# A two-layer attention and SwiGLU kernel: SyncE's DMA queue written in program order, weight loads set by the release of their slots, and the first half chunk's q and k evacuated straight into SBUF

## The chip, the cores and the metric

The kernel runs on one core of a Trainium2 chip. A core has TensorE (PE, matmuls), VectorE (DVE), ScalarE (ACT), GpSimd (POOL) and SyncE (SP, which here only issues DMA transfers). The metric is device time in microseconds (us), as a median of several executions. Spans inside a profile are about 1.8 us shorter than the time of the same execution. "Granted clock" is the share of TensorE's full clock that the profile shows as granted, 1.00 being all of it.

## The reference

Two layers. Each has a windowed attention (8 keys per token at distances 0, 2, ... 14; 32 heads of 32) and a SwiGLU block. S = 2048 tokens, D = 1024, F = 3584, all bf16.

```python
def _A_ref(x, wqkv, wo):
    qkv = (x @ wqkv).reshape(B, S, 3, H, Dh)          # then split into q, k, v
    logits = einsum("bhsd,bhswd->bhsw", q, k[idx]) * scale   # idx = pos - 2*w, masked below 0
    o = einsum("bhsw,bhswd->bhsd", softmax(logits), v[idx])
    return o.reshape(B, S, D) @ wo
def _B_ref(x, w1, w3, w2):
    return (silu(x @ w1) * (x @ w3)) @ w2
x = x + _A_ref(_layernorm(x), wqkv, wo);  x = x + _B_ref(_layernorm(x), w1, w3, w2)   # twice
```

## The kernel before

Tokens are handled in four chunks of 512 (`c`), and the attention in eight halves of 256 per layer (`h`). The engines share the work thus:

- TensorE computes q, k, v (`ps`, 8 tiles of 8 matmuls for each of q, k and v of a chunk), the output projection (`po`), gate and up (`pg`, `pu`) and the down projection (`acc`).
- ScalarE evacuates `ps`, which means that it copies the result out of the matmuls' accumulator into a staging tile `sgt`; SyncE stores `sgt` to DRAM and loads q, k, v of each half back as `qT`, `kT`, `vT`.
- VectorE does the attention itself: products with shifted copies of k, a tree of additions, softmax, products with shifted copies of v, giving `oT`. It also does layer norm statistics, residual additions and the SwiGLU product.

The instruction order of TensorE, VectorE and ScalarE is fixed by the program. The program keeps a small model of the three engines' times (`now`), and places background work of VectorE, and the `po` tiles, where that model believes their inputs ready. In the kernel before, the order of SyncE's queue is left to the scheduler of the framework. The code below is shortened, with comments added.

```python
ctx.enter_context(tc.manual_schedule(engines={PE, DVE, Activation}))      # SP is not in it
wp   = tile_pool(name="wp", bufs=8)      # 8 weight slots of 1 MB
qkvp = tile_pool(name="qkvp", bufs=1)    # qT, kT, vT: one buffer each
psum = tile_pool(name="psum", bufs=8)
...
def attention_steps():                   # a generator: each step is (cost, ready time, emit)
    for g, (l, h) in enumerate(halves):
        load_qk(l, h)                    # loads qT, kT if q and k of the chunk are stored
        while (l, h) not in qks: yield "blocked"; load_qk(l, h)
        load_v(l, h)                     # does nothing while v of the chunk is not stored
        ...                              # q*k products, softmax, At
        if g + 1 < len(halves): load_qk(*halves[g + 1])
        load_v(l, h)
        ...                              # At*v products -> oT
        oT_at[l, h] = now["dve"]
def between(hold, must=False):           # called between groups of TensorE's tiles
    while o_queue and (must or oT_at.get(half_of(o_queue[0]), 1e9) + 0.3 <= now["pe"]):
        o_tile()                         # 16 po matmuls
        if not must: break
...
for c in range(NCH):                     # the first layer's q, k, v
    for which in range(3):
        if c == NCH - 1 and which == 0: o_queue += [(0, n) for n in range(TPC)]
        if c == NCH - 1 and which == 2: between(False, True)     # the forced place
        q_part(0, c, which)
```

## Time and profile before

The time is 1634.05 us (median of 3, 1633.86 to 1635.31).

| what | value |
|---|---|
| span of the profiled execution | 1632.6 us |
| TensorE busy | 1614.9 us (99%) |
| VectorE busy | 1175.1 us (72%) |
| first `ps` matmul | 14.09 us |
| first `pg` matmul | 206.06 us |
| first attention product on VectorE | 60.08 us |

TensorE sets the time. The first lines below are the page's table of busy time by engine. The line after the dots is from its table of groups: line, engine, operation, output and inputs, shapes and count, then the busy time and mean ns of one, then the idle time before the group. "Busy" alone does not tell that TensorE runs at its peak. The count does, in the table of 25 us windows further down: 117 or 118 matmuls per full window, one each 0.216 us.

```profile
PE 1614.9 (99%) x7479; PEld 801.0 (49%) x7479; DVE 1175.1 (72%) x1960; ACT 351.9 (22%) x542; POOL 1.9 (0%) x12
...
L535 PE MATMUL pg<-xnT,w1t 128*128 128x512 bf16 x1792 | 423.3, 379 | 0.0
```

The table of windows of the kernel before: start and end of the window, its length, then busy us (and instructions) of PE, of the weight loads, of DVE, ACT and POOL, then the granted clock of TensorE, the DMA engines' busy share and GB/s.

```profile
150.00:175.00 25.00, 24.46 (x114) 15.42 (x113) 23.72 (x41) 9.30 (x17) 0.00 (x0) 1.00 0.43 117
175.00:200.00 25.00, 17.95 (x70) 8.70 (x69) 20.88 (x38) 3.60 (x7) 0.00 (x0) 0.80 0.71 227
200.00:225.00 25.00, 25.00 (x117) 12.60 (x116) 24.36 (x39) 8.53 (x12) 0.00 (x0) 1.00 0.76 234
```

The window from 175 to 200 us has 70 matmuls in place of 117, and a clock of 0.80. From 206 us on there is no listed wait of TensorE. The timeline of TensorE shows what happens there (start, duration, engine, line, operation, shapes, count, and in brackets the idle time before it and what ended it):

```profile
175.14 0.81 PE L466 MATMUL po<-wo,oT 128*128 128x512 bf16 x3
177.35 0.39 PE L466 MATMUL po<-wo,oT 128*128 128x512 bf16 x1 [1.41 <-DVE oT L317]
179.75 0.61 PE L466 MATMUL po<-wo,oT 128*128 128x512 bf16 x1 [2.01 <-DVE oT L317]
182.15 0.61 PE L466 MATMUL po<-wo,oT 128*128 128x512 bf16 x1 [1.79 <-DVE oT L317]
184.55 7.85 PE L466 MATMUL po<-wo,oT 128*128 128x512 bf16 x26 [1.79 <-DVE oT L317]
192.25 13.98 PE L500 MATMUL ps<-xnT,wqkv 128*128 128x512 bf16 x64
206.06 1.89 PE L535 MATMUL pg<-xnT,w1t 128*128 128x512 bf16 x8
```

TensorE reaches the `po` tiles of the second half and finds `oT` coming slice by slice from VectorE, 2.4 us apart. After that, 26 `po` matmuls take 7.85 us where 26 x 0.216 = 5.6 us would do: the clock had fallen. VectorE is late because it started late. These are the first three lines of the view of its waits between 14 and 206 us (what waited, for what: us in total, times, longest). The first of them lies mostly before the attention; the other two interrupt or delay it:

```profile
DVE rstd L202 <- ACT sd L195: 20.6, 7, 16.8
DVE pr L370 <- DMA kT<-qkv_d_1_127: 12.0, 1, 12.0
DVE xn L215 <- DMA xnT<-xn: 5.1, 2, 2.5
```

### The profile page before, as it was taken

The numbers are of one execution on the slowest core, as the hardware profiler recorded it, in microseconds if no ns is written. First come the engines' busy times: TensorE is split into PE (matmuls) and PEld (weight loads), VectorE is DVE, ScalarE is ACT, GpSimd is POOL, SyncE is SP. The second block draws the span as 40 slices with busy tenths as digits, with TensorE's granted clock in tenths as the row PEclk, the third lists the DMA queues.
The fourth block names the chain that finished last, engine by engine and source line by source line (L and its number), as shares of the span: only waits on it lengthen the run. The fifth ranks groups of instructions, "written<-read, shape, count | busy, mean of one in ns | idle before, by whom it ended". The sixth has DMA issues, their size and how long they took to land.

```text
span 1632.6 us, 18984 instructions
## 1 busy us (share of the span) xinstructions
PE 1614.9 (99%) x7479; PEld 801.0 (49%) x7479; DVE 1175.1 (72%) x1960; ACT 351.9 (22%) x542; POOL 1.9 (0%) x12
## 2 busy tenths in 40 slices
PE   8999899999999999999999999999999999999999
PEld 5666444444444644456444554445544444444444
DVE  3689899889998998999979848984489843122222
ACT  4332221204011331213222123022230212011110
POOL 0000000000000000000000000000000000000000
PEclk9999899999999999999999999999999999999999
DMA  9744664556646856477554674638675355445440
GB/s 313 223 126 129 194 194 146 166 168 191 186 154 180 258 158 180 142 220 247 154 169 143 200 252 143 181 129 256 222 183 163 123 178 168 142 143 180 155 129 27
DMA packets 337114, 286.33 MB, mean 175 GB/s; under 512 B 69632, under 2 KB 319488, under 8 KB 336896
## 3 DMA queue, kind: packets, MB, share of 16 engines
q1 hardware_dynamic: 336736, 284.59, 57.0%
q8 instruction: 58, 0.95, 0.2%
q10 hardware_dynamic: 288, 0.52, 0.1%
q14 instruction: 32, 0.26, 0.1%
HBM read 239.99 MB, written 29.36 MB: 165 GB/s over the span
## 4 chain that ended last, share of the span: by engine, by line
PE 94%; DVE 5%; DMA 1%; ACT 0%; issue 0%; ACTq 0%; DVEq 0%
PE acc L560 24%; PE pu L543 24%; PE pg L535 24%; PE ps L500 16%; PE po L466 6%; DVE pr L370 1%; DVE tm L429 1%; DVE pr L315 1%; DVE tm L315 1%; DMA xnT<-xn 0%; DVE psmT L393 0%; DVE L L395 0%; DMA x_sb<-in_A_x_dram 0%; DVE psm L317 0%; DVE st_133 L244 0%
## 5 line engine op out<-in xcount | busy, mean ns | idle before, releaser
L535 PE MATMUL pg<-xnT,w1t 128*128 128x512 bf16 x1792 | 423.3, 379 | 0.0
L543 PE MATMUL pu<-xnT,w3t 128*128 128x512 bf16 x1792 | 423.3, 379 | 0.0
L560 PE MATMUL acc<-w2t,hT 128*128 128x512 bf16 x1792 | 390.8, 379 | 0.0
L500 PE MATMUL ps<-xnT,wqkv 128*128 128x512 bf16 x1536 | 333.0, 379 | 2.3 <-ACT sgt L504 1.9
L539 ACT ACTIVATE sg<-pg 128x512 bf16<-128x512 f32 x224 | 133.7, 597 | 790.3 <-PE pg L535 755.7
L547 DVE TENSOR_TENSOR hT<-sg,pu 128x512 bf16<-128x512 bf16 x224 | 152.9, 683 | 209.9 <-PE pu L543 195.2
L543 PEld LDWEIGHTS <-w3t 128*128 128x128 bf16 x1792 | 175.3, 98 | 211.5
L560 PEld LDWEIGHTS <-hT 128*128 128x128 bf16 x1792 | 175.3, 98 | 211.5
L535 PEld LDWEIGHTS <-w1t 128*128 128x128 bf16 x1792 | 175.4, 98 | 211.4
L500 PEld LDWEIGHTS <-wqkv 128*128 128x128 bf16 x1536 | 220.4, 143 | 114.0 <-issue 2.9
L370 DVE TENSOR_TENSOR pr<-qT,kT 128x2048 bf16<-128x2048 bf16 x128 | 156.5, 1222 | 75.5 <-DMA kT<-qkv_d_1_130 61.2
L504 ACT CAST sgt<-ps 128x512 bf16<-128x512 f32 x192 | 109.1, 588 | 228.0 <-PE ps L500 195.8
L429 DVE TENSOR_TENSOR tm<-At,vT 128x2048 bf16<-128x2048 bf16 x128 | 156.2, 1220 | 2.4
L567 DVE TENSOR_TENSOR x_sb<-x_sb,acc 128x512 bf16<-128x512 bf16 x128 | 87.1, 681 | 91.4 <-PE acc L560 91.4
L315 DVE TENSOR_TENSOR pr<-pr 128x1024 bf16<-128x1024 bf16 (+1 forms) x256 | 134.4, 552 | 0.4
L315 DVE TENSOR_TENSOR tm<-tm 128x1024 bf16<-128x1024 bf16 (+1 forms) x256 | 133.4, 552 | 0.2
L466 PE MATMUL po<-wo,oT 128*128 128x512 bf16 x512 | 118.7, 384 | 7.0 <-DVE oT L317 7.0
L466 PEld LDWEIGHTS <-oT 128*128 128x128 bf16 x512 | 50.4, 99 | 69.9 <-DVE oT L317 9.3
L190 DVE BATCH_NORM_STATS2 st<-x_sb 128x6 f32<-128x512 bf16 x120 | 76.0, 671 | 0.3 <-DMA x_sb<-in_A_x_dram 0.3
L471 DVE TENSOR_TENSOR x_sb<-x_sb,po 128x512 bf16<-128x512 bf16 x64 | 43.3, 684 | 21.4 <-PE po L466 20.8
L539 ACT ACT_TABLE_LOAD x31 | 39.8, 1283 | 57.2 <-PE pg L535 57.1
L393 DVE STREAM_TRANSPOSE psmT<-psm 128x2048 bf16<-128x2048 bf16 x16 | 36.9, 2309 | 0.4
(160 smaller groups left out, 370.1 us busy)
## 6 DMA issues: line engine op xcount, KB each, us to landing
w1t<-in_B_w_dram SPq DMA_DIRECT2D x56, 1024.0 KB, 5.3
w3t<-in_B_w_dram SPq DMA_DIRECT2D x56, 1024.0 KB, 7.4
w2t<-in_B_w_dram SPq DMA_DIRECT2D x48, 1024.0 KB, 5.4
wqkv<-in_A_wqkv_dram SPq DMA_DIRECT2D x28, 1024.0 KB, 6.1
w2t<-in_B_w_dram SPq DMA_DIRECT2D x16, 512.0 KB, 5.1
qkv_d_0_126<-sgt SPq DMA_DIRECT2D x16, 256.0 KB, 2.8
qkv_d_1_127<-sgt SPq DMA_DIRECT2D x16, 256.0 KB, 5.3
qT<-qkv_d_0_126 SPq DMA_DIRECT2D x8, 512.0 KB, 4.8
```

Of the source, the lines that this page charges most:

```text
L315: nc.vector.tensor_tensor(b[:, 0:m, :], b[:, 0:m, :], b[:, m:2 * m, :], op=ALU.add)
L370: V.tensor_tensor(pr[:], qT[:], kT[:, :, k0:k0 + TCH], op=ALU.mult)
L429: V.tensor_tensor(tm[:], At[:], win, op=ALU.mult)
L466: nc.tensor.matmul(ps[:], lhsT=oT[:, t, j * P:(j + 1) * P], rhs=wo[:, t, hh * 512:(hh + 1) * 512], start=(t == 0), stop=(t == KT - 1))
L500: nc.tensor.matmul(ps[:], lhsT=ws[kk // KH][:, kk % KH, t::KT], rhs=xnT[:, kk, :], start=(kk == 0), stop=(kk == KT - 1))
L504: nc.scalar.copy(sgt[:, t - t0, :], ps[:])
L535: nc.tensor.matmul(pg[:], lhsT=w1t[:, kk, fi * P:(fi + 1) * P], rhs=xnT[:, kk, :], start=(kk == 0), stop=(kk == KT - 1))
L539: nc.scalar.activation(sg[:], pg[:], ACTF.Silu)
L543: nc.tensor.matmul(pu[:], lhsT=w3t[:, kk, fi * P:(fi + 1) * P], rhs=xnT[:, kk, :], start=(kk == 0), stop=(kk == KT - 1))
L547: nc.vector.tensor_tensor(hT[:, f - f0, :], sg[:], pu[:], op=ALU.mult)
L560: nc.tensor.matmul(acc[:], lhsT=hT[:, f - f0, j * P:(j + 1) * P], rhs=w2ts[(f - f0) // 8][:, (f - f0) % 8, :], start=(f == f0), stop=(f == ...
L567: nc.vector.tensor_tensor(xs, xs, acc[:], op=ALU.add)
```

## The change

Its intent: let the first attention begin as soon as k is computed, without a trip of q and k through DRAM, and keep SyncE's queue free of waits that hold other transfers back. There are also a fourth `xn` buffer (paid for by letting `L` and `An`, and `m4` and `e4`, share memory), other expected arrival times of x, and a first x tile that is split over two queues. Shortened to its core, with comments added:

```diff
-    ctx.enter_context(tc.manual_schedule(engines={PE, DVE, Activation}))
+    ctx.enter_context(tc.manual_schedule(engines={PE, DVE, Activation, SP}))
-    x_at = [12.5] + [20.0 + 10 * c for c in range(1, NCH)]
+    x_at = [12.5, 22.0, 27.0, 36.0]
-    for j in range(TPC):
-        (nc.scalar if j % 2 else nc.sync).dma_start(x_sb[:, j:j + 1, :], xin[:, j:j + 1, :])
+    for j, queue in ((0, nc.sync), (1, nc.sync), (TPC - 1, nc.scalar), (2, nc.sync)):
+        for h in range(2 if j == 0 else 1):        # tile 0 in two halves, one per queue
+            ...
+    seq = [...]        # all weight tiles, in the order of their use
+    def load_weight(pieces=1): ...                 # next tile of seq, on SyncE's queue
+    def release(n): due.extend([None] * n)         # after a tile's last matmul
+    def flush():                                   # first thing in between()
+        while due: due.pop(); load_weight()
 def q_part(...):
+        first = (l, c) == (0, 0) and which < 2
+        if first: now_T = qkvp.tile(..., name="kT" if which else "qT"); ...
                 nc.scalar.copy(sgt[:, t - t0, :], ps[:])
+                if first:
+                    nc.scalar.copy(now_T[:, t, HALO if which else 0:], ps[:, 0:TCH])
...
-    load_wqkv(0, 2)
-    load_x(1)
-    load_wqkv(1)
-    load_wqkv(2)
+    for i in range(4):                             # the weights of q and k
+        load_weight(1 if i > 1 else 2)
+    load_x(1)
...                                                # v's weights, x of chunks 2 and 3: inside q of chunk 0
             if c == 1 and which == 1:
-                nc.sync.dma_start(wo[:], wo_v)
+                then = (lambda: nc.sync.dma_start(wo[:], wo_v),)
```

More of the change, by code (lines that the diff above doesn't have):

```diff
@@ L65 @@
     wp = ctx.enter_context(tc.tile_pool(name="wp", bufs=8))
-    xnp = ctx.enter_context(tc.tile_pool(name="xn", bufs=3))
+    xnp = ctx.enter_context(tc.tile_pool(name="xn", bufs=4))
     xtp = ctx.enter_context(tc.tile_pool(name="xnT", bufs=2))
@@ L77 @@
     ctx.enter_context(tc.manual_schedule(engines={mybir.EngineType.PE, mybir.EngineType.DVE,
-                                                  mybir.EngineType.Activation}))
+                                                  mybir.EngineType.Activation, mybir.EngineType.SP}))
     MM, TABLE, DMA = 0.216, 1.3, 2.5
@@ L160 @@
     x_sb = const.tile([P, S // P, D], BF16, name="x_sb")
-    for j in range(TPC):
-        (nc.scalar if j % 2 else nc.sync).dma_start(x_sb[:, j:j + 1, :], xin[:, j:j + 1, :])
+    for j, queue in ((0, nc.sync), (1, nc.sync), (TPC - 1, nc.scalar), (2, nc.sync)):
+        for h in range(2 if j == 0 else 1):
+            w_ = D // (2 if j == 0 else 1)
+            (nc.scalar if h else queue).dma_start(x_sb[:, j, h * w_:(h + 1) * w_], xin[:, j, h * w_:(h + 1) * w_])
     hT = const.tile([P, HTN, CH], BF16, name="hT")
@@ L376, in attention_steps @@
             psmT = smp.tile([P, W * NE, 4], BF16, name="psmT", tag="tr")
-            L = smp.tile([P, W, NE], FP32, name="L")
-            m4 = smp.tile([P, 4, NE], FP32, name="m4")
+            L = smp.tile([P, W, NE], FP32, name="L", tag="L")
+            m4 = smp.tile([P, 4, NE], FP32, name="m4", tag="m4")
             mx = smp.tile([P, NE], FP32, name="mx")
             E = smp.tile([P, W, NE], BF16, name="E")
-            e4 = smp.tile([P, 4, NE], FP32, name="e4")
             sm_ = smp.tile([P, NE], FP32, name="sm_")
@@ L384, in attention_steps @@
             rsb = smp.tile([P, NE], BF16, name="rsb")
-            An = smp.tile([P, W, NE], BF16, name="An")
             at = {}
@@ L401, in attention_steps @@
             yield 0.72, 0.0, exps
+            e4 = smp.tile([P, 4, NE], FP32, name="e4", tag="m4")
+            An = smp.tile([P, W, NE], BF16, name="An", tag="L")
             yield 0.46, at["E"], lambda: V.tensor_tensor(e4[:], E[:, 0:4, :], E[:, 4:8, :], op=ALU.add)
@@ L440, with load_weight @@
     KH = KT // 2
-    wq_held = {}
-    def load_wqkv(which, pieces=1):
-        halves = []
-        for h in range(2):
+    NW = 8
+    seq = [("qkv", which, h) for which in range(3) for h in range(2)]
+    for u in range(len(units)):
+        for f0, f1 in fsplits:
+            for g0 in range(f0, f1, FG):
+                seq += [("w1", g0, min(FG, f1 - g0)), ("w3", g0, min(FG, f1 - g0))]
+            seq += [("w2", g0, min(8, f1 - g0), hh) for hh in range(2) for g0 in range(f0, f1, 8)]
+        if 1 <= u and u + 3 < len(units):
+            seq += [("qkv", which, h) for which in range(3) for h in range(2)]
+    w_tiles, due, used = [], [], [0]
+    def load_weight(pieces=1):
+        if len(w_tiles) == len(seq):
+            return
+        kind, i, n, *rest = seq[len(w_tiles)]
+        if kind == "qkv":
             w = wp.tile([P, KH, D], BF16, name="wqkv", tag="w")
@@ L450, in load_wqkv, with weight, release @@
                 nc.sync.dma_start(w[:, k0:k0 + step, :],
-                                  wqkv_v[:, h * KH + k0:h * KH + k0 + step, which * D:(which + 1) * D])
-            halves.append(w)
-        wq_held[which] = halves
+                                  wqkv_v[:, n * KH + k0:n * KH + k0 + step, i * D:(i + 1) * D])
+        elif kind == "w2":
+            w = wp.tile([P, 8, 512], BF16, name="w2t", tag="w")
+            nc.sync.dma_start(w[:, 0:n, :], w2_v[:, i:i + n, rest[0] * 512:(rest[0] + 1) * 512])
+        else:
+            w = wp.tile([P, KT, FG * P], BF16, name=kind + "t", tag="w")
+            v = w1_v if kind == "w1" else w3_v
+            nc.sync.dma_start(w[:, :, 0:n * P], v[:, :, i * P:(i + n) * P])
+        w_tiles.append(w)
+    def weight(kind):
+        w = w_tiles[used[0]]
+        assert seq[used[0]][0] == kind
+        used[0] += 1
+        return w
+    def release(n):
+        due.extend([None] * n)
+    def flush():
+        while due:
+            due.pop()
+            load_weight()
     o_queue, norm_queue = [], []
@@ L477, in between @@
     def between(hold, must=False):
+        flush()
         while o_queue and (must or oT_at.get((o_queue[0][0], o_queue[0][1] // 2), 1e9) + 0.3 <= now["pe"]):
@@ L488, in ready_norm, with q_part @@
         return xnT_at[key]
-    def q_part(l, c, which):
+    firsts = []
+    def q_part(l, c, which, ws, then=()):
         ready = ready_norm(("Q", l, c))
         xnT = xnTs[("Q", l, c)]
-        ws = wq_held[which]
+        first = (l, c) == (0, 0) and which < 2
+        if first:
+            now_T = qkvp.tile([P, KT, TCH + (HALO if which else 0)], BF16, name="kT" if which else "qT")
+            firsts.append(now_T)
+            if which:
+                nc.vector.memset(now_T[:, :, 0:HALO], 0.0)
         for t0 in range(0, KT, SG):
@@ L505, in q_part @@
                 done = act(0.6, r)
+                if first:
+                    nc.scalar.copy(now_T[:, t, HALO if which else 0:], ps[:, 0:TCH])
+                    done = act(0.4)
             nc.sync.dma_start(qkv_d[l][which][:, t0:t0 + SG, c * CH:(c + 1) * CH], sgt[:])
             between(False)
+            if then and t0 // SG < len(then):
+                then[t0 // SG]()
         qkv_at[l, c, which] = done + DMA / 2
+        if len(firsts) == 2:
+            qks[0, 0] = firsts[0], firsts[1], done + 0.1
+            firsts.append(None)
     def b_stage(u, hold):
@@ L519, in b_stage @@
                 gn = min(FG, f1 - g0)
-                w1t = wp.tile([P, KT, FG * P], BF16, name="w1t", tag="w")
-                nc.sync.dma_start(w1t[:, :, 0:gn * P], w1_v[:, :, g0 * P:(g0 + gn) * P])
-                w3t = wp.tile([P, KT, FG * P], BF16, name="w3t", tag="w")
-                nc.sync.dma_start(w3t[:, :, 0:gn * P], w3_v[:, :, g0 * P:(g0 + gn) * P])
+                w1t, w3t = weight("w1"), weight("w3")
                 for fi in range(gn):
@@ L528, in b_stage @@
                         between(hold)
+                    else:
+                        flush()
                     if f == 8 and 1 <= u and u + 3 < len(units):
@@ L548, in b_stage @@
                     th = dve(0.64, r)
+                release(2)
             for hh in range(2):
-                w2ts = []
-                for g0 in range(f0, f1, 8):
-                    gn = min(8, f1 - g0)
-                    w2t = wp.tile([P, 8, 512], BF16, name="w2t", tag="w")
-                    nc.sync.dma_start(w2t[:, 0:gn, :], w2_v[:, g0:g0 + gn, hh * 512:(hh + 1) * 512])
-                    w2ts.append(w2t)
+                w2ts = [weight("w2") for g0 in range(f0, f1, 8)]
                 for j in range(TPC):
@@ L570, in b_stage @@
                         nc.sync.dma_start(xout[:, n, hh * 512:(hh + 1) * 512], xs)
+                    if j == TPC - 1:
+                        release(2)
                     between(hold and not lastsplit, lastsplit and hh == 0 and j == 1 and not hold)
@@ L578 @@
     xnT_at["Q", 0, 0], norm_left["Q", 0, 0] = now["pe"], 0
-    load_wqkv(0, 2)
+    for i in range(4):
+        load_weight(1 if i > 1 else 2)
     load_x(1)
-    load_wqkv(1)
-    load_wqkv(2)
-    for r in range(R):
-        queue_norm(("Q", 0, 1), 1, r)
+    queue_norm(("Q", 0, 1), 1, 0)
+    queue_norm(("Q", 0, 1), 1, 1)
+    for c in (2, 3):
+        for r in range(R):
+            queue_norm(("Q", 0, c), c, r, (norm_stats,))
     for c in range(NCH):
@@ L590 @@
                 between(False, True)
-            q_part(0, c, which)
-            if c == 0 and which < 2:
-                load_x(2 + which)
-                for r in range(R):
-                    queue_norm(("Q", 0, 2 + which), 2 + which, r, (norm_stats,))
+            then = ()
+            if c == 0 and which == 0:
+                then = (lambda: load_x(2), load_weight, load_weight, lambda: load_x(3))
+            if c == 1 and which == 0:
+                then = (load_weight, load_weight)
             if c == 1 and which == 1:
-                nc.sync.dma_start(wo[:], wo_v)
+                then = (lambda: nc.sync.dma_start(wo[:], wo_v),)
+            q_part(0, c, which, w_tiles[2 * which:2 * which + 2], then)
+            if c == NCH - 1:
+                release(2)
             if which == 0 and 1 <= c < NCH - 1:
@@ L600 @@
                     queue_norm(("Q", 0, c + 1), c + 1, r, (norm_apply,))
+    used[0] = 6
     for u, (l, c) in enumerate(units):
@@ L609 @@
             for which in range(3):
-                load_wqkv(which)
                 if which == 2:
                     between(False, True)
-                q_part(*units[q], which)
+                q_part(*units[q], which, [weight("qkv"), weight("qkv")])
+                release(2)
 _INS = ['A_x', 'A_wqkv', 'A_wo', 'B_x', 'B_w1', 'B_w3', 'B_w2']
```

## The prediction

> **What bounds the kernel now.** TensorE. The page's busy table gives it 99% of the 1632.6 us span. From the first `pg` matmul (206.06 us, timeline of PE) to the end, no wait of PE is listed, and the table of 25 us windows shows 117 or 118 matmuls in every window after 200 us: one per 0.216 us. The Trainium skill ("TensorE: Matmul & The Clock Gate", phases on the wall clock) states 215.7 ns for a warm 512-column matmul; this trace agrees, so nothing is to be gained after 206 us.
>
> What can be gained lies before 206 us:
> - Head: the first `ps` matmul starts at 14.09 us. VectorE waits 3.9 us for the first x tile (view of waits); the serial norm chain runs from there.
> - 14.09 to 206.06 is 191.97 us, with 768 `ps` and 64 `po` matmuls: 832 x 0.216 = 179.7 us. So 12.3 us are lost. The view of waits names `po <- DVE oT` 7.0 us in 4 waits (177 to 185 us), `ps <- ACT sgt` 1.9 us (98 and 154 us). The rest, about 3 us, is the clock: in windows of 4 us the granted clock is 0.79, 0.50, 0.50, 0.93 between 176 and 192 us. The same page (HAM oscillation) warns of idle gaps over 3.4 us; here four of 1.4 to 2.0 us sufficed.
>
> **What the change does.**
> 1. q and k of the first half chunk go straight to SBUF. Before, VectorE sat 12.0 us until `kT` returned from DRAM, started attention at 60.08 us, broke off for 6.6 us of statistics, and lost 5.1 us to `xn` waiting for the transposes. From 60.08 to 185.07 (second half's `oT`) is 125 us, so 113 us without those two. Now k's last tile is copied about 28.7 us after the first `ps` matmul, near 42 us, with all statistics done in the idle time before. The second `oT` then ends near 155 us; the forced `po` tiles need it near 171 us. The wait goes, and its throttling.
> 2. Cost: 16 more ScalarE copies of 128x256, about 0.4 us each (estimated from the 0.59 us copy). ScalarE then does about 1.0 us per 1.73 us tile: hidden.
> 3. SyncE in program order and weight loads at release: stores of `sgt` should no longer stand behind transposes that wait, so the 1.9 us should go. After 206 us loads were already early enough: no gain. Risk: a DMA waiting for VectorE holds weights back, but the prefetch is three pairs of tiles (about 40 us) deep.
> 4. x tile 0 in two halves on two queues: the head shrinks by about 0.9 us.
>
> **Sum.** -12.3 -0.9, plus about 1 us given back: the built-in schedule takes `po` tiles as soon as its model thinks `oT` is done, and VectorE's measured step (2.40 us) is longer than modelled (2.295 us), so one short wait may appear near 155 us. Predicted 1621.8 us, ratio 0.9925; range 1618.5 to 1626. Faster by over 2%: 0.01; within 2%: 0.98; slower by over 2%: 0.01.
>
> **Right if** the first attention product starts at 41 to 44 us, the first `pg` near 193 to 195 us, the `po` wait is under 3 us, the granted clock stays at 1.0 from 20 us on, and windows after 200 us are unchanged. **Wrong if** a new wait of PE for a weight tile or for `sgt` appears (SyncE blocked behind VectorE), if early x chunks land late and stop ScalarE's evacuations at 15 to 45 us.

## The result, and the profile after

The changed kernel takes 1627.83 us (median of 4, 1626.79 to 1628.48); in the same rounds the kernel before took 1634.68 us. The ratio is 0.9957, with a 95% interval of 0.9940 to 0.9975: a gain of 0.4%, where 0.75% was predicted. Ratios here are the mean time of one kernel's runs over that of the other's of the same rounds, so they are not quite the ratio of the medians. Executions over 1.5% slower than the fastest of the same kernel are left out of the means. With 2% as the threshold, the two kernels count as equally fast; the interval still excludes a ratio of 1.

The profile after spans 1626.7 us. The first `ps` starts at 13.04 us and the first `pg` at 200.26 us. The same two views of the changed kernel, windows first:

```profile
150.00:175.00 25.00, 20.82 (x85) 11.62 (x85) 24.69 (x46) 5.66 (x10) 0.00 (x0) 0.90 0.42 121
175.00:200.00 25.00, 24.89 (x110) 15.30 (x111) 23.16 (x42) 6.10 (x12) 0.00 (x0) 0.96 0.72 199
200.00:225.00 25.00, 24.89 (x115) 11.37 (x116) 22.83 (x35) 9.70 (x13) 0.00 (x0) 1.00 0.77 235
```

Some matmul records are missing from this trace (7330 of 7479), so 115 stands for a full window. Then the timeline of TensorE in the changed kernel:

```profile
164.98 1.34 PE L500 MATMUL po<-wo,oT 128*128 128x512 bf16 x5
168.33 0.39 PE L500 MATMUL po<-wo,oT 128*128 128x512 bf16 x1 [2.01 <-DVE oT L319]
170.73 4.68 PE L500 MATMUL po<-wo,oT 128*128 128x512 bf16 x10 [2.01 <-DVE oT L319]
175.21 4.50 PE L542 MATMUL ps<-xnT,wqkv 128*128 128x512 bf16 x16
...
200.26 1.89 PE L584 MATMUL pg<-xnT,w1t 128*128 128x512 bf16 x8
```

The wait for `oT` did not go. It is 4.0 us instead of 7.0, and matmuls after it are slow again: 10 `po` in 4.68 us where 2.2 would do. From 13.04 to 200.26 us is 187.22 us for 832 matmuls, which take 179.6 us when nothing stops them (measured in experiment 1 below). So 7.6 us are lost; before, it was 191.97 - 179.6 = 12.4.

VectorE tells why. The first three lines of the view of its waits between 14 and 206 us in the changed kernel:

```profile
DVE tm L431 <- DMA vT<-qkv_d: 11.6, 1, 11.6
DVE rstd L204 <- ACT sd L197: 7.0, 7, 2.9
DVE st L192 <- DMA x_sb<-in_A_x_dram: 6.9, 1, 6.9
```

The waits for `kT` and for the transposes are gone, as predicted. A wait of 11.6 us for `vT` is new. The timeline of SyncE and VectorE in the changed kernel shows it being made:

```profile
76.44 0.47 SPq L646 DMA_DIRECT2D wo<-in_A_wo_dram  x1
...
79.87 0.63 SPq L338 DMA_DIRECT2D qT<-qkv_d  x1
80.56 3.87 SPq L338 DMA_DIRECT2D kT<-qkv_d  x1
80.93 0.11 DVE L335 MEMSET vT<- 128x64 uint32 x1
84.47 2.87 SPq L336 DMA_DIRECT2D vT<-qkv_d  x1
...
92.63 1.23 DVE L431 TENSOR_TENSOR tm<-At,vT 128x2048 bf16<-128x2048 bf16 x1 [11.59 <-DMA vT<-qkv_d]
```

v of chunk 0 had been computed by about 55 us. But the program, before and after the change, asks for `vT` in two places only: at the start of a half (where it does nothing for the first half, because the program has not yet placed v's tiles) and after the softmax. In program order the load therefore stands behind the softmax's place, behind 2 MB of `wo` and behind the next half's `qT` and `kT`. In the kernel before, the scheduler had moved both loads forward. The timelines of SyncE and VectorE in the kernel before show it:

```profile
44.07 0.57 SPq L597 DMA_DIRECT2D wo<-in_A_wo_dram  x1
...
67.96 0.53 SPq L334 DMA_DIRECT2D vT<-qkv_d_2_128  x1
...
103.84 0.11 DVE L333 MEMSET vT<- 128x64 uint32 x1
```

The program clears the edge of `vT` (the MEMSET) just before it issues the load, and VectorE keeps program order; so the MEMSET at 103.84 us marks the load's place in the program. The scheduler had put the load 36 us ahead of it, and it landed long before VectorE needed it at 104 us. `wo`, which the program requests after k of chunk 1 (its matmuls end near 83 us), went out at 44.07 us.

The second `oT` was predicted near 155 us and ended at 171.3. Attention started at 46.66 us, which is 4.7 us later than the 42 us predicted, and the wait for `vT` took 11.6 us: together 16.3 us, the whole difference.

### The profile page after: what moved, and what is told of

The parts are those of the page before. It is cut to its first block, busy times and chain, and to the rows that moved or that the text cites. A ratio compares the mean times of both kernels' runs of the same rounds, so it can differ in the third digit from the quotient of the medians.

```text
span 1626.7 us, 18858 instructions
## 1 busy us (share of the span) xinstructions
PE 1608.2 (99%) x7330; PEld 801.3 (49%) x7479; DVE 1174.2 (72%) x1960; ACT 357.0 (22%) x558; POOL 1.9 (0%) x12
## 4 chain that ended last, share of the span: by engine, by line
PE 93%; DVE 5%; DMA 1%; issue 1%; SPq 0%; ACT 0%; DVEq 0%
PE pu L592 24%; PE acc L605 24%; PE pg L584 24%; PE ps L542 15%; PE po L500 6%; DVE tm L431 1%; DVE tm L317 1%; DVE pr L372 1%; DMA vT<-qkv_d 0%; DVE pr L317 0%; SPq L338 0%; DMA x_sb<-in_A_x_dram 0%; DVE oT L319 0%; DVE xn L217 0%; DVE x_sb L505 0%
## 5 line engine op out<-in xcount | busy, mean ns | idle before, releaser
L542 PEld LDWEIGHTS <-wqkv 128*128 128x128 bf16 x1536 | 220.5, 144 | 113.0 <-issue 2.1
```

What stands on the lines that cost most here:

```text
L542: nc.tensor.matmul(ps[:], lhsT=ws[kk // KH][:, kk % KH, t::KT], rhs=xnT[:, kk, :], start=(kk == 0), stop=(kk == KT - 1))
```

## The experiments

Eleven kernels ran, each in rounds of five with the kernel before on the same chip. The kernel before took 1633.96, 1633.88 and 1634.39 us in the three groups (median of 9 each). Each kernel has five runs, experiment 1 four. All results were correct. Every edit below is against the changed kernel unless said otherwise. Theory A: the place of the `vT` load in SyncE's queue delays VectorE, and that makes TensorE wait. Rival B: VectorE simply starts too late and has too much to do. Rival C: the DMA engines are full then, whatever the order.

### 1. The vT load right after v is stored (e1_v_early)

```diff
             q_part(0, c, which, w_tiles[2 * which:2 * which + 2], then)
+            if c == 0 and which == 2:
+                load_v(0, 0)
```

> The changed kernel with one move: the load of the first half's vT is put on SyncE's queue right after v's last store of chunk 0, instead of after the first half's softmax. Theory A (the late place of this load in the queue costs the 11.6 us wait of VectorE, and that makes the second oT late for the po tiles): the vT wait at 81 to 93 us goes to under 1 us, the second oT is done near 159.5 us instead of 171.0, the po wait of 4.0 us and the throttling after it go or shrink to one wait of under 2 us; first pg near 193 to 196 us instead of 200.3, time 1620 to 1623 us (changed kernel 1627.8). Rival B (VectorE's work itself is too long and the late start of attention at 46.7 us decides): the po wait stays near 4 us and the time above 1626 us. Rival C (the DMA engines are full at that time, whatever the order): vT still lands after 88 us.

Measured: 1620.61 us (1620.53 to 1620.68), ratio 0.9918 (0.9905 to 0.9932). `vT` was issued at 57.3 us and is no wait. The second `oT` ended at 161.1 us. No wait of TensorE is left between 14 and 210 us. Its timeline in this run:

```profile
161.33 3.62 PE L500 MATMUL po<-wo,oT 128*128 128x512 bf16 x16
164.79 3.62 PE L542 MATMUL ps<-xnT,wqkv 128*128 128x512 bf16 x16
168.24 3.62 PE L500 MATMUL po<-wo,oT 128*128 128x512 bf16 x16
171.69 20.88 PE L542 MATMUL ps<-xnT,wqkv 128*128 128x512 bf16 x96
192.41 1.89 PE L584 MATMUL pg<-xnT,w1t 128*128 128x512 bf16 x8
```

From the first `ps` at 12.84 to 192.41 us is 179.57 us for the 832 matmuls, or 215.8 ns each. The Trainium skill ("TensorE: Matmul & The Clock Gate", phases on the wall clock) gives 215.7 ns per warm 512-column matmul, so nothing is lost here. Theory A holds; B and C fall as sole causes. Attention still started at 46.5 us here, so the late start alone cost TensorE nothing. The margin is thin, though: `oT` came 1.6 us later than expected, and the `po` tile was taken 0.2 us after `oT` was done.

### 2. wo loaded later (e2_wo_late)

```diff
-            if c == 1 and which == 1:
+            if c == 2 and which == 0:
                 then = (lambda: nc.sync.dma_start(wo[:], wo_v),)
```

> The changed kernel with the 2 MB load of wo moved from chunk 1's k to chunk 2's q, so that it no longer stands right before the loads of qT, kT and vT. Theory A (the place of the vT load after the softmax is the cause; wo only lengthens it): vT is still issued only after the softmax, at 81 us or later, but lands in about 5 us instead of 8.1 and is not held up in its issue (kT 3.9 us, vT 2.9 us of issue before): the wait falls from 11.6 us to about 5 or 6 us, the second oT comes near 165 us, time 1623 to 1626 us. Rival C (wo's traffic is all of it): the wait falls to 2 us or less, and the time is that of the run with the early load, near 1621 us.

Measured: 1621.81 us, ratio 0.9926 (0.9914 to 0.9939). `vT` was issued at 81.0 us, still after the softmax, and was waited for 7.3 us, more than the 5 to 6 expected. `kT`'s issue took 0.7 us instead of 3.9. The second `oT` ended at 166.7 us, and TensorE's wait shrank to 0.3 us, because its `po` tile at 164.68 us uses the slices of `oT` as they come. So the load stays late without `wo` in front of it, as A says, and `wo` added 4.3 us to the wait. The time missed the range expected under A (1623 to 1626 us) and lies near the 1621 us that rival C expected; but C also expected a wait of 2 us or less, and that did not come. Taking away 4.3 of 11.6 us already bought 6.0 of the 7.2 us that experiment 1 bought: TensorE's loss is not proportional to the delay, because it begins only where `oT` comes later than its `po` tile.

### 3. Only the direct evacuation (e3_direct_only)

Against the kernel before; the scheduler still chooses SyncE's order, and nothing else in the program is changed. The diff is cut: the lines that make `qT` and `kT` and register them are left out.

```diff
                 nc.scalar.copy(sgt[:, t - t0, :], ps[:])
+                if first:
+                    nc.scalar.copy(now_T[:, t, HALO if which else 0:], ps[:, 0:TCH])
```

> The kernel before, with the direct evacuation of the first half's q and k as its only change; SyncE's queue stays in the order that the scheduler chose, x loads as before. Theory A: attention starts near 43 to 47 us instead of 60.1, vT is issued near 68 us as before and is no wait, the second oT comes near 165 to 170 us instead of 185, the po wait of 7.0 us goes mostly: saves 8 to 12 us, so 1623 to 1627 us. If the queue in program order is needed for the gain, the time stays above 1631 us.

Measured: 1626.86 us, ratio 0.9956 (0.9944 to 0.9969): as much as the whole change. The first `ps` started at 13.60 us instead of 14.09, and no wait for `sgt` is listed, so some of the gain lies outside the attention. Attention started only at 53.2 us (expected 43 to 47), held by statistics in the old order; `vT` was issued at 61.4 us and was no wait; the second `oT` ended at 178.1 us (expected 165 to 170), and the `po` wait was 3.7 us. The time was as expected, the path to it was not; that the time fell into the range is partly luck.

### 4. Only the rest: order, weights, x, buffers (e4_order_only)

```diff
-        first = (l, c) == (0, 0) and which < 2
+        first = False
```

> The changed kernel without the direct evacuation: q and k of the first half go through DRAM again, on SyncE's queue in program order. Theory A (the order alone buys only the head's 1.05 us; the gain comes from the direct evacuation, and the order delays vT): attention starts near 50 us or later, the vT wait shrinks because the softmax comes later, the second oT comes at 170 to 178 us; time 1628 to 1634 us. Rival (the order buys what was gained): time within 1 us of the changed kernel's 1627.8 us.

Measured: 1632.26 us, ratio 0.9990 (0.9977 to 1.0004), not clear of noise. Attention started at 49.0 us, `vT` was waited for 10.3 us, the second `oT` ended at 172.6 us, and the `po` wait was 7.5 us, most of it (5.75 us) one wait, since a tile was taken at 162.56 us. So the rest of the change brought the start of attention forward by 11 us, and gave that back in the wait for `vT` and in a tile taken too early. I had expected the `vT` wait to shrink; it fell only from 11.6 to 10.3 us. The parts of this rest were not tried one by one, apart from the head (experiment 8).

### 5. The waiting filled with matmuls on zeros (e5_fill)

```diff
             for t in range(KT):
+                if (l, n, hh) == (0, 2, 0):
+                    warm({5: 9, 6: 10, 7: 2}.get(t, 0))
```

> The changed kernel with 21 matmuls on zeros put into the po tile that waits (9, 10 and 2 of them before its sixth, seventh and eighth product), so that TensorE works instead of idling; oT comes when it came. Theory A (the 4.0 us of waiting cost about 3.6 us more, because the idle gaps throttle the clock): the granted clock stays at 1.0 from 164 to 180 us, the waited time stays near 4 to 4.5 us, first pg near 196.5 us instead of 200.3, time 1623.5 to 1625 us. Rival (the slow matmuls after the wait are slow for another reason, such as weights or PSUM): the time stays within 1 us of 1627.8 us.

Measured: 1625.69 us, ratio 0.9949 (0.9936 to 0.9961), 0.7 us above the expected range. The granted clock stayed at 1.00. The windows of the changed kernel, then of this run:

```profile
168.00:172.00 4.00, 1.60 (x4) 0.48 (x5) 3.93 (x9) 0.00 (x0) 0.00 (x0) 0.77 1.02 284
172.00:176.00 4.00, 4.00 (x10) 1.41 (x9) 3.97 (x8) 0.00 (x0) 0.00 (x0) 0.50 1.08 361
```

```profile
168.00:172.00 4.00, 3.93 (x19) 1.46 (x18) 3.93 (x10) 0.00 (x0) 0.00 (x0) 1.00 1.03 260
172.00:176.00 4.00, 4.00 (x20) 2.33 (x20) 3.97 (x6) 0.13 (x1) 0.00 (x0) 1.00 1.09 365
```

The second window has 20 matmuls instead of 10. From first `ps` to first `pg` it took 184.90 us instead of 187.22. Here the slow matmuls after the wait are thus caused by the wait itself: 2.3 of the 7.6 us lost. I had expected 3.6, by taking all that the listed waits left over. The 2.3 us is the difference of one profiled execution of each kernel; the intervals of the two ratios overlap, so the size is less sure than the clock. Of the 5.3 us still lost, the 21 extra matmuls take 21 x 0.216 = 4.5 us, in place of the waiting for slices of `oT`.

### 6. The po tiles held to the forced place (e6_forced)

```diff
-        while o_queue and (must or oT_at.get(...) + 0.3 <= now["pe"]):
+        while o_queue and (must or o_queue[0] not in ((0, 2), (0, 3)) and oT_at.get(...) + 0.3 <= now["pe"]):
```

> The changed kernel with one change on TensorE's order: the po tiles of the second half may not be taken early, only at the forced place before v of chunk 3, near 172 us. The vT load stays late (wait of VectorE near 11.6 us, second oT near 171 us). Theory A2 (the late vT hurts only because the built-in schedule, which believes oT earlier than it comes, takes a po tile at 165 us): the po wait goes to under 1 us, first pg near 192.5 to 193.5 us, time 1620.5 to 1622 us. Rival (a late oT costs its lateness wherever the tile stands): time stays at 1625 us or more.

Measured: 1623.02 us, ratio 0.9931 (0.9918 to 0.9943), 1 us above the expected range. `vT` was waited for 11.9 us and the second `oT` ended at 171.7 us, as in the changed kernel. Yet no `po` wait is listed before the first `pg`, because the tiles stood at 171.98 us, 0.3 us after `oT` was done. The first `pg` came at 194.47 us, so 1.8 us were lost. In exchange TensorE waited 1.6 us for ScalarE at the first `pg`: ScalarE's queue had a square root waiting 6.8 us for VectorE's statistics, with evacuations behind it. So the late `oT` cost 7.6 us only together with a schedule that believed it ready at 165 us. The model of times allows 2.5 us for a load; `vT` took 8.1 us from issue to landing.

### 7. Statistics earlier (e7_stats_early)

```diff
-    x_at = [12.5, 22.0, 27.0, 36.0]
+    x_at = [12.5, 15.5, 24.0, 33.0]
     for i in range(4):
+        if i == 2: load_x(1)
         load_weight(1 if i > 1 else 2)
-    load_x(1)
```

> The changed kernel with x of chunk 1 loaded before k's weights, and the schedule told of it (chunks 1 to 3 expected at 15.5, 24 and 33 us instead of 22, 27 and 36), so that all statistics end sooner. Theory A (attention starts at 46.7 instead of 42 us because the statistics of chunks 1 to 3 are not done; the vT load follows the softmax in the queue and waits behind wo, qT and kT): attention starts at 42 to 44.5 us; vT still lands after 86 us, so its wait stays at 9 us or more and the second oT comes no more than 4 us earlier, near 167 to 170 us; the po wait shrinks to 0 to 3 us, time 1621 to 1627 us. Rival (the start of attention was the whole of the delay): vT's wait falls by itself and the second oT comes near 160 us.

Measured: 1639.33 us, ratio 1.0030 (1.0017 to 1.0042): slower than the kernel before, and outside everything expected. Attention started at 50.7 us. The timeline of SyncE in this run shows the transposes now standing in front of x of chunk 3:

```profile
21.53 5.93 SPq L220 DMA_TRANSPOSE xnT<-xn  x2
27.55 0.53 SPq L551 DMA_DIRECT2D qkv_d<-sgt  x1
28.14 0.46 SPq L463 DMA_DIRECT2D wqkv<-in_A_wqkv_dram  x1
28.69 6.60 SPq L220 DMA_TRANSPOSE xnT<-xn  x2
35.39 0.53 SPq L551 DMA_DIRECT2D qkv_d<-sgt  x1
35.97 0.46 SPq L622 DMA_DIRECT2D x_sb<-in_A_x_dram  x1
```

x of chunk 3 was issued at 35.97 us (28.07 in the changed kernel), VectorE waited 9.7 us for it, and TensorE waited 9.3 us for ScalarE's evacuations near 100 and 143 us. In this trace, each transfer starts only when the pair of transposes ahead of it has been issued. The pairs did not wait for VectorE: it had written their inputs by 20.50 and 25.68 us. Why a pair took 5.9 and 6.6 us, when most later pairs take 2.7, no run shows.

### 8. Only the split of the first x tile (e8_head_only)

Against the kernel before: only the loop over the first four x loads is that of the change.

> The kernel before with only the first x loads changed (tile 0 in two halves on two queues, then tiles 1, 3 and 2). Theory: the first ps matmul starts at 12.7 to 13.1 us instead of 14.1, as in the changed kernel; with the second oT bound by VectorE, which starts its attention when kT has come through DRAM, part of the shift may be lost in a longer po wait: time 1632.5 to 1634 us. Rival (the order of the weight loads or the schedule makes the head shorter): the start stays at 14.0 us.

Measured: 1634.53 us, ratio 1.0001 (0.9988 to 1.0015). This is 0.5 us above the expected range. The first `ps` matmul started at 12.74 us instead of 14.09, but the first `pg` at 206.38 us. Attention still began when `kT` came from DRAM, at 59.85 us (60.08 before), and the second `oT` ended at 184.9 us (185.2 before). The wait for `oT` was again 7.0 us, and 3.0 us were spent waiting for `sgt` (1.9 before). The head's gain is real, and here, where `oT` decides when the stage ends, it was worth nothing.

### 9. x of chunk 1 ahead of k's weights (e9_x_first)

```diff
     for i in range(4):
+        if i == 2: load_x(1)
         load_weight(1 if i > 1 else 2)
-    load_x(1)
```

> The changed kernel with x of chunk 1 loaded before k's weights and nothing else. It tells apart two reasons for the start of attention at 46.7 us instead of 42. If the late landing of x (19.9 us, behind 4 MB of weights) is the reason, attention starts at 43 us or before. If it is the place of the square roots in ScalarE's order (the first comes at 24.3 us, the second at 31.3 us, between evacuations), x lands near 14.4 us but the statistics still wait for them and attention starts at 46 to 47 us; then vT's wait, the second oT (171 us) and the time (1626 to 1628.5 us) stay as in the changed kernel.

Measured: 1627.57 us, ratio 0.9957 (0.9945 to 0.9970), the same as the changed kernel. The timeline of VectorE in this run:

```profile
14.68 1.29 DVE L192 BATCH_NORM_STATS2 st<-x_sb 128x6 f32<-128x512 bf16 x2 [1.90 <-DMA x_sb<-in_A_x_dram]
...
24.42 0.17 DVE L204 RECIPROCAL rstd<-sd 128x2 f32<-128x2 f32 x1 [6.74 <-ACT sd L197]
```

x came 5.2 us earlier, and attention started at 46.4 us as before. The time went into waiting for `sd`, a square root that ScalarE does between evacuations, at 24.1 us, though its input was there at 17.6. The Trainium skill ("TensorE: Matmul & The Clock Gate", architectural detail) calls ScalarE's and VectorE's queues strictly first in, first out; the trace agrees. So an earlier x of chunk 1 does not bring attention forward: the square root's place in ScalarE's program holds the statistics back. That moving the square roots is enough was not shown; experiments 7 and 11 moved them and met other obstacles.

### 10. vT early and wo late together (e10_v_and_wo)

The edits of experiments 1 and 2 together.

> The changed kernel with both the early vT load and the later wo load: does anything remain before the first pg? If TensorE's count is the floor (832 matmuls of 0.216 us are 179.7 us after a start near 12.9 us), it is no faster than the run with the early vT load alone: 1620.0 to 1621.2 us, no po wait, first pg near 192.5 us. If there is still a wait to be gained, below 1619.5 us.

Measured: 1620.61 us, ratio 0.9917 (0.9904 to 0.9931), equal to experiment 1, with the first `pg` at 192.34 us. Nothing more was to be had in this stage.

### 11. Statistics earlier, x of chunk 3 ahead of the transposes (e11_stats_early2)

```diff
-  then = (lambda: load_x(2), load_weight, load_weight, lambda: load_x(3))
+  then = (lambda: (load_x(2), load_x(3)), load_weight, load_weight)      # on top of experiment 7
```

> As the run that took the statistics earlier and came out slower (its load of chunk 3's x stood behind transposes on SyncE's queue until 36.0 us and landed at 43), but with the load of chunk 3's x issued together with chunk 2's, ahead of the transposes. If that blocking was the reason of its failure, x is no wait of VectorE after 16 us, attention starts at 41.5 to 44 us, and no wait of TensorE for evacuations of more than 1 us comes near 98 us. For the changed kernel's 16 us of lateness it tells what the 4.7 us of late start were worth: if the vT load swallows an earlier start, vT's wait grows to 13 us or more and the second oT stays at 168 us or later; if not, the second oT comes near 166 us and the time is 1621 to 1624 us. If x's late load was not the reason, the time stays above 1630 us.

Measured: 1633.67 us, ratio 0.9998 (0.9986 to 1.0011). VectorE's wait for x fell to 2.3 us, as expected, but attention started at 45.65 us (expected 41.5 to 44): the pair of transposes now occupied SyncE for 9.4 us (21.5 to 30.9 us), stores of `sgt` stood behind it, and ScalarE waited for their buffers (57.8 us in 14 waits up to 210 us). TensorE waited 4.9 us for evacuations, and 3.9 us for `oT`, which ended at 167.4 us. By the rule set beforehand, a time above 1630 us speaks against x as the reason of experiment 7's failure. Since the time fell by 5.7 us all the same, x was one obstacle of experiment 7; the trace shows the transposes as another. What a start of attention at 42 us would be worth was not isolated and stays open.

## Why the prediction was wrong, point by point

- **What bounds the kernel: right.** TensorE's count outside the first 206 us is unchanged, and the time fell by what the first stage lost less: 206.06 - 200.26 = 5.8 us of 5.9 us of span.
- **Step 1, "The second `oT` then ends near 155 us ... The wait goes, and its throttling": this is the step that failed.** It ended at 171.3 us. The 113 us for VectorE's work were about right: 171.3 - 46.7 - 11.6 = 113.0, and 114.6 in experiment 1. What was wrong is the idle time in between, which the prediction set at zero. The `vT` load moves behind the softmax when SyncE goes by program order: 11.6 us. Taking that wait away (experiment 1) removes TensorE's wait and its throttling, as the mechanism says, and gives 1620.61 us. That this is close to the predicted 1621.8 is partly luck: `oT` ended at 161.1 us there, not at 155, and its `po` tile was taken just 0.2 us later.
- **Attention "near 42 us, with all statistics done in the idle time before": wrong by 4.7 us.** The last copy of k ended at 41.7 us, as predicted; the statistics were not done. They wait for square roots that stand between evacuations in ScalarE's order (experiment 9).
- **"The forced po tiles need it near 171 us": the wrong deadline.** A tile was taken at 165 us, at the place where the built-in model believed `oT` ready. The prediction named this risk and put 1 us on it. With `oT` 16 us later than predicted, the loss was 7.6 us; with the tiles held to the forced place it was 1.8 us (experiment 6).
- **Step 2, ScalarE's extra copies: right.** They took 0.38 us each, and TensorE does not wait for them.
- **Step 3, "-1.9 us" for `sgt`: right, and the listed risk was too narrow.** The waits for `sgt` are gone. The prediction looked for blocked weights and stores, and did not ask of each load when the program first asks for it.
- **Step 4, the head: right in size (1.05 us against 0.9), wrong as a term of a sum.** In the kernel before, it buys nothing alone (experiment 8). It can count only where `oT` no longer decides, as in experiment 1; it was not tried alone there.
- **"-12.3 us" in total: it was -4.75 us,** from 12.4 lost to 7.6.

The direct evacuation accounts for the gain by itself (experiment 3). The rest of the change, alone, is not clear of noise (experiment 4). Together they bring no more than the first alone, because the new order adds the `vT` wait.

The version of experiment 1 beats both kernels: 1620.61 us, 0.8% under the kernel before, with two lines more than the changed kernel.

## What to carry to other kernels

When you take a queue from a scheduler and give it program order, go through every load on it and ask at which line the program first requests it: the scheduler may have been moving it forward for you. When a producer's time lies near a consumer's place, a delay costs nothing up to a threshold and several us beyond it, and a static schedule that believes the producer early moves the threshold against you; so look for the slack, not only for the sum of waits. A gain ahead of such a wait, as in the head here, is worth nothing until the wait is gone.

## What the Trainium skill lacked or had wrong

- "TensorE: Matmul & The Clock Gate" gives about 3.4 us without work as what throttles the clock. Here two listed waits of 2.01 us with one matmul between them were followed by 4 us at a granted clock of 0.50, and filling them kept it at 1.00. The page also says, under its second failure mode, that frequent short idles make the clock oscillate, but not how short; 2.01 us is such a length.
- "DMA: Bandwidth & Descriptors": I found no figure for how long an issue occupies SyncE when much is outstanding. `kT`'s issue took 3.9 us shortly after 2 MB of `wo` and 0.7 us without it. A pair of transposes took 2.7 us in most places, but 7.4 us at 28.6 us and 8.0 us at 189.2 us in the changed kernel, and 9.4 us in experiment 11.
